# An attention, softmax-MLP and cosine-MLP kernel: the last 64 keys of a late pair are transposed without padding, and the priorities of its list scheduler get other values

## The chip, the cores and the metric

One core of one Trainium2 chip runs the whole program. The metric is device time in microseconds of one execution. The kernel before took 796.75 us (median of three runs, 796.06 to 797.55).

## What is computed

Three layers in a row, all in float32: causal attention in blocks of 64 (4 batches, 8 heads, 576 positions, head size 64), an MLP with a softmax-weighted activation and a layer norm, and an MLP whose activation is h * cos(h). The weights of the MLPs come as float64.

```python
scores = scale * np.matmul(q, k.transpose(0, 1, 3, 2))
mask = block_i >= block_j                  # blocks of 64 positions
scores = np.where(mask, scores, -1000000000.0)
attn = np.exp(scores - np.max(scores, axis=-1, keepdims=True))
attn = attn / (np.sum(attn, axis=-1, keepdims=True) + 1e-09)
o = np.matmul(attn, v)                     # -> x: 2304 tokens x 512

h = x @ w_in                               # 512 -> 1024
sm = softmax(h)
solu = h * sm
ln = (solu - mean) / np.sqrt(var + 1e-06) * g_ln
y = ln @ w_out                             # 1024 -> 512

h = y @ w2_in                              # 512 -> 2048
out = (h * np.cos(h)) @ w2_out             # 2048 -> 512
```

## The kernel before

**Tiles.** Attention works on pairs of heads. A pair's 576 queries are split in two: a *late* group (the last 320 queries, all 576 keys) and an *early* group (the first 256 queries, 256 keys). There are 8 groups (the four late ones first, then the four early ones, `groups`) of 4 pairs each, 16 late and 16 early pairs in all. A late pair has three units (`trace_unit`, t = 2, 3, 4): two of 128 queries and one, t = 4, that puts the last 64 queries of both heads on 128 partitions, with 576 keys in the free dimension. Each unit is a chain: scores on PE (L495 and L498, or L530 for t = 4), the row maximum on DVE, exponentials on ACT, a normalisation on whichever of three engines (L524), PE transposes of the probabilities (L581, in pieces of up to four 128x128 blocks per PSUM bank), a copy to `eT`; then one product with the values for the pair (`trace_pv`, L606).

For t = 4 the 576 keys are four blocks of 128 and one of 64. The tile `e` is 640 wide, its last 64 columns are set to zero (L537, on POOL or DVE), the fifth block is transposed as 128 columns, and only partitions 0 to 63 of the result are copied out.

The 2304 tokens then go in 18 tiles of 128 through the first MLP: `trace_l1` (L678, 24 matmuls of 512 columns), the activation and norm, transposes (`trace_lnT`, L711), and for each four tiles the second matmul in four parts d (`trace_l2`, L732). The second MLP runs over 5 chunks of tokens and 16 weight tiles in two halves: `trace_h2` (L771), the cosine chain on ACT and DVE (`trace_cos`), `trace_out` (L811). The float64 weights are turned into pairs of float32r tiles by `trace_weight` (ACT, DVE and POOL, POOL's part being L641). Attention output goes into a ring of five token tiles (`xs`, slot n % 5), so attention can be at most five tiles ahead of `trace_l1`.

**What sets the order.** All operations are recorded first. `Scheduler.run` then plays a greedy list schedule with costs that are written beside each operation: whenever an engine is free, it takes the ready operation with the smallest key, and the instructions are issued on each engine in that order. The key is `prio - off`. `prio` comes from a time line (`att_iv`, `tile_pr`, `end1` = 373.8 us worked out from its constants) minus or plus the entries of the table `P`; `off` is taken from `P` too, by engine and kind of work:

```python
if kinds & {"e1", "LN", "yb", "psh", "st"}:
    return P["mlp_pe"] if e == "p" else P["mlp_vec"]
if kinds & {"e", "eT", "us", "rq", "rk", "rv", "xs"}:
    return (P["att_pe"] if e == "p" else P["att_vec"]) - P["att_slope"] * o.prio
```

An attention pair of group gi has `prio = s + l * p / 4 - P["lead<gi>"] - P["pair"][p]`, token tile n has `tile_pr[n] + P["tile"][n]`, part d of the second matmul adds `P["l2"] + P["l2_step"] * d`, the weight tiles of the second MLP have `end1 + P["w2_direct"] + P["w2_step"] * (2 * f + c)`. A tile in SBUF or PSUM is given to an operation when it starts, if a slot is free; matmuls on a spare bank (L953) fill planned gaps in the first 70 us.

Of the kernel before, what the change touches and what calls it, by code (L numbers as in the profile page):

```python
# [10 lines left out]
F32 = mybir.dt.float32  # L11
# [17 lines left out]


P = {
    "stick": 24783.0,
    "tile": [-14359.3, -37985.7, 6113.4, -3055.7, 24465.2, 4623.7, 3526.9, -32896.1, -22525.7, 27230.1, -18199.6, 22478.0, 37632.5, 59648.4, -15097.6, 596.8, -22562.3, -32058.0],
    "pair": [-10908.6, 3875.9, 1648.0, 792.0],
    "weight": {"p": 1.0, "s": 2.385, "v": 2.75, "g": 1.376, "q": 1.0},
    "att_slope": 0.053,
    "att_pe": 74866.7,
    "att_vec": 151894.2,
    "mlp_pe": -14159.9,
    "mlp_vec": 34158.7,  # L40
    "w_in": -10429.3,
    "w_out": 307495.7,
    "w_out_step": 1138.4,
    "w2_direct": 73027.9,
    "w2_step": 12920.1,
    "lead0": 7512.5,
    "lead1": 22625.7,
    "lead2": 8969.7,
    "lead3": -7974.6,
    "lead4": -9446.8,  # L50
    "lead5": -67400.4,
    "lead6": -7144.6,
    "lead7": -13408.6,
    "l2": 5241.5,
    "l2_step": 15170.5,
    "prep": 36287.5,
}


# [12 lines left out]
class Scheduler:  # L72
# [24 lines left out]
    def op(self, engs, fn, r=(), w=(), prio=0.0, port=False, iss=0.0, kind="M"):  # L97


        o = Op()  # L100
        o.engs, o.fn, o.prio, o.port, o.iss, o.kind = engs, fn, prio, port, iss, kind
        o.idx, o.succ, o.pred, o.ready, o.start = len(self.ops), [], [], {}, None
        deps, tiles = set(), []
        for k in list(r) + list(w):
            t = k[0] if isinstance(k, tuple) else k
            if isinstance(t, Lt) and t not in tiles:
                tiles.append(t)
        for k in r:
            if k in self.last_w:
                deps.add(self.last_w[k])  # L110
        for k in w:
            if k in self.last_w:
                deps.add(self.last_w[k])
            deps.update(self.reads.get(k, ()))
        for k in r:
            self.reads.setdefault(k, []).append(o)
        for k in w:
            self.last_w[k] = o
            self.reads[k] = []
        deps.discard(o)  # L120
        o.ndep = len(deps)
        for d in deps:
            d.succ.append(o)
        for t in tiles:
            t.refs += 1
        o.tiles = tiles
        self.ops.append(o)
        return o
# [163 lines left out]
def fused_kernel(ctx: ExitStack, tc: tile.TileContext, qT, kT, vm, vt, w_in, w_out, g_ln, w2_in, w2_out, out):  # L292
    nc = tc.nc
    V, S, G, PE = nc.vector, nc.scalar, nc.gpsimd, nc.tensor
# [7 lines left out]
    op = sch.op  # L302


    def c_s(n, ap=False, acc=False):
        return 0.833 * n + 93 + (93 if ap else 0) + (93 if acc else 0)

    def c_v(n):
        return 1.04 * n + 65
# [48 lines left out]
    ident = const.tile([128, 128], F32, name="ident")  # L358
# [102 lines left out]
    def trace_unit(i, t, prep, eT, prio):  # L461
        gi, p = gp_list[i]
        g = groups[gi][1]
        rq, rk, rv = prep
        q0 = g_q0(gi)
        W = 128 * (t + 1)
        us = Lt("us", [128, 8], F32)
        if g == 0:
            if t == 0:
                first_e[i] = [Lt("e", [128, 2, 128 * x + 128], F32) for x in range(2)]  # L470
            e = first_e[i][t]
        else:
            e = Lt("e", [128, 2, W] if t < 4 else [128, 640], F32)

        row = g == 0
        rows = [slice(64 * h, 64 * h + 64) for h in range(2)]
# [49 lines left out]
        else:  # L526
# [5 lines left out]
            for c in range(2):  # L532
# [1 line left out]
                   [scl[c]], [(us, c)], prio)  # L534
            op({"v": 130}, lambda _: V.tensor_scalar(out=us.ap[:, 2:3], in0=us.ap[:, 0:1], scalar1=us.ap[:, 1:2], scalar2=None, op0=ALU.min),
               [(us, 0), (us, 1)], [(us, 2)], prio, port=True)
            op({"g": 130, "v": 100}, lambda q: (V if q == "v" else G).memset(e.ap[:, 576:640], 0.0), [(us, 2)], [(e, 2)], prio)  # L537
            for c in range(2):
                op({"s": c_s(288, True, True)}, lambda _, c=c: S.activation(
                    e.ap[:, 288 * c:288 * c + 288], scl[c].ap, AF.Exp, bias=us.ap[:, 2:3], scale=1.0, accum_out=us.ap[:, 4 + c:5 + c]),  # L540
# [17 lines left out]
        pieces = []  # L558
        if t < 2:
            src = [(h, 128 * j) for h in range(2) for j in range(t + 1)]  # L560
            o = 0 if t == 0 else 128
            pieces.append(([lambda h=h, a=a: e.ap[:, h, a:a + 128] for h, a in src], [(e, 0), (e, 1)],
                           lambda ps: ps.rearrange("p (h q) -> p h q", h=2), lambda x: x[:, :, o:o + W], (t,)))
        elif t < 4:
            for h in range(2):
                o = 128 * (t - 2)
                pieces.append(([lambda h=h, j=j: e.ap[:, h, 128 * j:128 * j + 128] for j in range(t + 1)], [(e, h)],
                               lambda ps: ps.rearrange("p (j q) -> p j q", q=128),
                               lambda x, h=h, o=o: x[:, h, :].rearrange("p (j q) -> p j q", q=320)[:, 0:t + 1, o:o + 128], (t, h)))
        else:  # L570
            pieces.append(([lambda j=j: e.ap[:, 128 * j:128 * j + 128] for j in range(4)], [(e, 0), (e, 1)],
                           lambda ps: ps.rearrange("p (j h q) -> p j h q", j=4, h=2),
                           lambda x: x.rearrange("p h (j q) -> p j h q", q=320)[:, :, :, 256:320], (4,)))
            pieces.append(([lambda: e.ap[:, 512:640]], [(e, 0), (e, 1), (e, 2)], None, None, (5,)))
        for srcs, rk_, vps, vdst, key in pieces:
            n = len(srcs)
            ps = Lt("psb", [128, 128 * n], F32)

            def f_t(_, srcs=srcs, ps=ps):
                for k, s in enumerate(srcs):  # L580
                    PE.transpose(ps.ap[:, 128 * k:128 * k + 128], s(), ident)  # L581
            op({"p": 109 * n}, f_t, rk_ + [(eT, "a")], [ps], prio, kind="T")
            if vps is None:
                f_p, f_d, m = lambda ps=ps: ps.ap[0:64].rearrange("p (h q) -> p h q", h=2), lambda: eT.ap[0:64, :, 960:1024], 128
            else:
                f_p, f_d, m = lambda ps=ps, vps=vps: vps(ps.ap), lambda vdst=vdst: vdst(eT.ap), 128 * n
            op({"s": c_s(m), "v": c_v(m)}, lambda q, f_p=f_p, f_d=f_d: copy(q, f_d(), f_p()), [ps], [(eT,) + key], prio)
# [273 lines left out]
    for i, (gi, p) in enumerate(gp_list):  # L861
        us = (0, 1) if groups[gi][1] == 0 else (2, 3, 4)
        s_, l_ = att_iv[gi]
        pr = s_ + l_ * p / NPAIR - P[f"lead{gi}"] - P["pair"][p]
        prep = trace_prep(i, pr - P["prep"])
        n = 384 if groups[gi][1] == 0 else 1280
        eT = Lt("eT", [128, 2, n], F32)
        for k, t in enumerate(us):
            trace_unit(i, t, prep, eT, pr + l_ / NPAIR * k / len(us))
        trace_pv(i, prep, eT, pr + l_ / NPAIR)  # L870
# [8 lines left out]
    for n in range(NT):  # L879
        pr = tile_pr[n] + P["tile"][n]  # L880
        e = trace_l1(n, pr)
# [18 lines left out]
    for k in range(len(slots) + LAG):  # L900
        if k < len(slots):
            q, c, f = slots[k]
# [6 lines left out]
        if k >= LAG:  # L909
            q, c, f = slots[k - LAG]  # L910
# [20 lines left out]
    with tc.manual_schedule():  # L931
# [9 lines left out]
        for o in order:  # L941
            for t in o.tiles:
                if t.ap is None:
                    make, k, gate, _ = sch.classes[t.cls][t.slot]
# [42 lines left out]
```

## Time and profile before

| | us |
|---|---|
| median of three runs | 796.75 |
| the profiled execution | 796.97 |
| its span, first to last instruction | 795.2 |
| PE (matmul) busy | 784.4 |
| DVE busy | 588.0 |
| ACT busy | 421.8 |
| POOL busy | 219.2 |

The 1.8 us between span and time of the profiled execution lie outside its instructions. PE's busy time is a union of pipelined matmuls, each recorded longer than the distance to its successor, so a PE that waits 0.1 us between two of them is still shown as busy. For this reason the distance between the starts of two groups of matmuls is read beside the busy share.

### The profile page before, as it was taken

The numbers are of one execution on the slowest core, as the hardware profiler recorded it, in microseconds if no ns is written. First come the engines' busy times: TensorE is split into PE (matmuls) and PEld (weight loads), VectorE is DVE, ScalarE is ACT, GpSimd is POOL, SyncE is SP. The second block draws the span as 40 slices with busy tenths as digits, with TensorE's granted clock in tenths as the row PEclk, the third lists the DMA queues.
The fourth block names the chain that finished last, engine by engine and source line by source line (L and its number), as shares of the span: only waits on it lengthen the run. The fifth ranks groups of instructions, "written<-read, shape, count | busy, mean of one in ns | idle before, by whom it ended". The sixth has DMA issues, their size and how long they took to land.

```text
span 795.2 us, 12231 instructions
## 1 busy us (share of the span) xinstructions
PE 784.4 (99%) x4291; PEld 622.1 (78%) x4291; DVE 588.0 (74%) x1238; ACT 421.8 (53%) x944; POOL 219.2 (28%) x320
## 2 busy tenths in 40 slices
PE   8999999999999999999999999999999999999998
PEld 5566666767888777889887778889988888888996
DVE  6989998664643774689879999667766676767775
ACT  6987997655433784476354555343434333333332
POOL 2675544412111553555634542000000000000000
PEclk9999999999999999999999999999999999999999
DMA  8435433322112221624385423022415032131121
GB/s 284 155 96 193 138 109 127 109 79 68 41 53 99 81 68 40 234 104 146 115 300 207 133 85 127 11 100 75 149 51 196 3 109 78 54 132 43 51 79 41
DMA packets 46030, 86.79 MB, mean 109 GB/s; under 512 B 4240, under 2 KB 18576, under 8 KB 45968
## 3 DMA queue, kind: packets, MB, share of 16 engines
q1 hardware_dynamic: 45968, 86.00, 32.5%
q8 instruction: 34, 0.56, 0.3%
q14 instruction: 28, 0.23, 0.1%
HBM read 67.11 MB, written 18.87 MB: 108 GB/s over the span
## 4 chain that ended last, share of the span: by engine, by line
PE 86%; DVE 4%; DMA 3%; ACT 2%; POOL 2%; issue 1%; SPq 0%; ACTq 0%; POOLq 0%
PE banks L771 22%; PE banks L811 22%; PE banks L732 13%; PE banks L678 11%; PE banks L606 6%; PE banks L581 5%; PE banks L495 4%; DMA rq<-qT 3%; PE banks L530 2%; PE banks L711 2%; POOL e L524 1%; DVE tr L787 1%; DVE gt L336 1%; DMA rw<-w_out 1%; POOL t L641 0%
## 5 line engine op out<-in xcount | busy, mean ns | idle before, releaser
L678 PE MATMUL banks<-w,XS 128*128 128x512 f32 x432 | 110.5, 401 | 0.0
L331 ACT ACTIVATE gt<-ta 128x512 fp32r<-128x512 f32 (+1 forms) x80 | 47.0, 588 | 110.0 <-PE banks L811 72.0
L732 PE MATMUL banks<-LN,w 128*128 128x512 f32 (+1 forms) x480 | 103.8, 372 | 0.0
L732 PEld LDWEIGHTS banks<-LN,w 128*128 128x128 f32 x480 | 83.1, 189 | 15.1 <-DVE LN L336 0.2
L678 PEld LDWEIGHTS banks<-w,XS 128*128 128x128 f32 x432 | 78.0, 188 | 18.6 <-issue 3.4
L811 PE MATMUL banks<-w,gt 128*128 128x512 f32 x378 | 91.8, 390 | 0.0
L641 POOL TENSOR_TENSOR t<-t,rw 128x512 uint32<-128x512 uint32 x45 | 63.8, 1419 | 80.3 <-DVE t L639 21.4
L782 ACT ACTIVATE ta<-banks 128x512 f32<-128x512 f32 (+1 forms) x80 | 44.3, 554 | 77.5 <-PE banks L771 76.0
L811 PEld LDWEIGHTS banks<-w,gt 128*128 128x128 f32 x378 | 70.8, 188 | 14.1
L783 DVE TENSOR_SCALAR ta<-ta 128x512 f32<-128x512 f32 (+1 forms) x80 | 37.1, 463 | 59.3 <-ACT ta L782 59.1
L509 ACT ACTIVATE e<-banks,us 128x384 f32<-128x384 f32 (+3 forms) x128 | 66.3, 530 | 20.0 <-DVE us L506 18.0
L791 ACT ACTIVATE ta<-tr,hpi 128x512 f32<-128x512 f32 (+1 forms) x80 | 53.9, 673 | 37.5 <-DVE tr L789 37.4
L506 DVE TENSOR_REDUCE us<-banks 128x1 f32<-128x384 f32 (+3 forms) x128 | 56.0, 481 | 14.8 <-PE banks L498 11.0
L336 DVE TENSOR_TENSOR gt<-ta,gt 128x512 fp32r<-128x512 f32 (+1 forms) x80 | 54.0, 675 | 16.4 <-ACT gt L331 15.6
L811 PE MATMUL banks<-wa,gt 128*128 128x512 f32 x270 | 65.7, 390 | 0.0
L792 DVE TENSOR_TENSOR ta<-banks,ta 128x512 f32<-128x512 f32 (+1 forms) x80 | 50.8, 636 | 12.3 <-ACT ta L791 11.9
L581 PE MATMUL banks<-ident,e 128*128 128x128 f32 x400 | 58.7, 278 | 1.1 <-POOL e L524 0.7
L524 POOL TENSOR_SCALAR e<-e,us 128x384 f32<-128x384 f32 (+3 forms) x97 | 49.1, 518 | 37.8 <-ACT e L509 20.4
L331 ACT ACTIVATE eT<-banks 128x512 f32<-128x512 f32 (+3 forms) x104 | 50.4, 525 | 16.0 <-PE banks L581 15.3
L811 PEld LDWEIGHTS banks<-wa,gt 128*128 128x128 f32 x270 | 50.5, 188 | 10.1
L581 PEld LDWEIGHTS banks<-ident,e 128*128 128x128 f32 x400 | 45.4, 140 | 16.0 <-POOL e L524 4.5
L787 DVE SCALAR_TENSOR_TENSOR tr<-ta,tr 128x512 f32<-128x512 f32 (+1 forms) x80 | 55.3, 692 | 2.2
(127 smaller groups left out, 1428.9 us busy)
## 6 DMA issues: line engine op xcount, KB each, us to landing
rw<-w_out SPq DMA_DIRECT2D x24, 512.0 KB, 3.6
rw<-w_in SPq DMA_DIRECT2D x22, 512.0 KB, 3.9
yD<-YB SPq DMA_DIRECT2D x16, 512.0 KB, 2.9
wa<-yD SPq DMA_DIRECT2D x7, 1024.0 KB, 7.6
rk<-kT SPq DMA_DIRECT2D x16, 288.0 KB, 3.7
oD<-ob SPq DMA_DIRECT2D x18, 256.0 KB, 2.4
ob<-oD SPq DMA_DIRECT2D x18, 256.0 KB, 3.3
rv<-vm SPq DMA_DIRECT2D x16, 256.0 KB, 2.9
```

Source lines behind the costliest of these rows:

```text
L331: S.activation(dst, src, AF.Copy, scale=1.0 if scale is None else scale)
L336: (V if eng == "v" else G).tensor_tensor(out=dst, in0=src, in1=h.bitcast(F32), op=ALU.subtract)
L506: op({"v": c_v(W)}, lambda _, h=h: V.tensor_reduce(out=us.ap[:, h:h + 1], in_=scs[h](), axis=AX.X, op=ALU.max, negate=True), [keys[h]], [( ...
L509: op({"s": c_s(W, True, True)}, lambda _, h=h: S.activation(e.ap[:, h, :], scs[h](), AF.Exp, bias=us.ap[:, h:h + 1], scale=1.0, accum_out= ...
L524: G.tensor_scalar(out=a, in0=a, scalar1=us.ap[:, 6 + h:7 + h], scalar2=1.0, op0=ALU.mult, op1=ALU.mult)
L581: PE.transpose(ps.ap[:, 128 * k:128 * k + 128], s(), ident)
L641: op({"g": c_g2(512)}, lambda _: G.tensor_tensor(out=t1.ap, in0=t1.ap, in1=lw(), op=ALU.add), [(rw, 0)], [t1], prio)
L678: PE.matmul(h.ap[:, 512 * c:512 * c + 512], lhsT=xs.ap[:, a, kt, :], rhs=w[:, b, 512 * c:512 * c + 512], start=(kt == 0 and a == 0 and b = ...
L732: PE.matmul(y.ap, lhsT=w[:, a], rhs=LN[:, b, kf, s0_:s0_ + len(t), :], start=(kf == 0 and a == 0 and b == 0), stop=(kf == 7 and b == 1))
L771: PE.matmul(ps.ap, lhsT=w[:, a, 128 * kt:128 * kt + 128], rhs=yts[q, c][kt // 2].ap[:, kt % 2, b, :], start=(k == 0), stop=(k == 11))
L787: op({"v": c_v(n)}, lambda _: V.scalar_tensor_tensor(out=r.ap, in0=a.ap, scalar=-TWO_PI_B, in1=r.ap, op0=ALU.mult, op1=ALU.add), [a], [r], ...
L811: PE.matmul(acc[x][1](), lhsT=gt.ap[:, a, 128 * x:128 * x + 128], rhs=w[:, b, 512:1024], start=(f % 8 == 0 and k == 0), stop=(f % 8 == 7 a ...
```

## The change

In the unit t = 4 of a late pair the tile `e` becomes 576 wide, the memset of the padding is dropped, and the fifth block is transposed with its 64 columns only; the transpose then writes partitions 0 to 63 of the bank. Its cost in the list schedule becomes 70 instead of 109. All entries of `P` get other values.

```diff
 P = {
-    "stick": 24783.0,
-    "tile": [-14359.3, -37985.7, 6113.4, -3055.7, 24465.2, 4623.7, 3526.9, -32896.1, -22525.7, 27230.1, -18199.6, 22478.0, 37632.5, 59648.4, -15097.6, 596.8, -22562.3, -32058.0],
-    "pair": [-10908.6, 3875.9, 1648.0, 792.0],
-    "weight": {"p": 1.0, "s": 2.385, "v": 2.75, "g": 1.376, "q": 1.0},
-    "att_slope": 0.053,
-    "att_pe": 74866.7,
-    "att_vec": 151894.2,
-    "mlp_pe": -14159.9,
-    "mlp_vec": 34158.7,
-    "w_in": -10429.3,
-    "w_out": 307495.7,
-    "w_out_step": 1138.4,
-    "w2_direct": 73027.9,
-    "w2_step": 12920.1,
-    "lead0": 7512.5,
-    "lead1": 22625.7,
-    "lead2": 8969.7,
-    "lead3": -7974.6,
-    "lead4": -9446.8,
-    "lead5": -67400.4,
-    "lead6": -7144.6,
-    "lead7": -13408.6,
-    "l2": 5241.5,
-    "l2_step": 15170.5,
-    "prep": 36287.5,
+    "stick": 26451.6,
+    "tile": [-43245.2, -107671.1, -30339.0, -14639.2, -22911.6, 4197.5, -31824.9, -26533.9, -797.8, 49077.2, -9719.6, 28521.2, 35640.7, 57607.5, -32409.5, 12744.3, 18745.8, -13140.0],
+    "pair": [-728.0, 7631.2, 6406.5, 9082.1],
+    "weight": {"p": 1.0, "s": 2.732, "v": 2.775, "g": 1.38, "q": 1.0},
+    "att_slope": 0.104,
+    "att_pe": 87074.2,
+    "att_vec": 82748.2,
+    "mlp_pe": -25868.9,
+    "mlp_vec": -41636.5,
+    "w_in": -13390.0,
+    "w_out": 317764.2,
+    "w_out_step": 30356.0,
+    "w2_direct": 410330.0,
+    "w2_step": 6619.4,
+    "lead0": 9930.6,
+    "lead1": 13443.4,
+    "lead2": -18192.8,
+    "lead3": -900.9,
+    "lead4": 18506.1,
+    "lead5": -39857.0,
+    "lead6": -10385.0,
+    "lead7": -29368.1,
+    "l2": 12436.2,
+    "l2_step": 4011.6,
+    "prep": 28608.8,
 }
...
-            e = Lt("e", [128, 2, W] if t < 4 else [128, 640], F32)
+            e = Lt("e", [128, 2, W] if t < 4 else [128, 576], F32)
...
-            op({"g": 130, "v": 100}, lambda q: (V if q == "v" else G).memset(e.ap[:, 576:640], 0.0), [(us, 2)], [(e, 2)], prio)
...
-            pieces.append(([lambda: e.ap[:, 512:640]], [(e, 0), (e, 1), (e, 2)], None, None, (5,)))
+            pieces.append(([lambda: e.ap[:, 512:576]], [(e, 0), (e, 1)], None, None, (5,)))
...
-            def f_t(_, srcs=srcs, ps=ps):
+            def f_t(_, srcs=srcs, ps=ps, vps=vps):
                 for k, s in enumerate(srcs):
-                    PE.transpose(ps.ap[:, 128 * k:128 * k + 128], s(), ident)
-            op({"p": 109 * n}, f_t, rk_ + [(eT, "a")], [ps], prio, kind="T")
+                    PE.transpose(ps.ap[0:64 if vps is None else 128, 128 * k:128 * k + 128], s(), ident)
+            op({"p": 109 * n if vps else 70}, f_t, rk_ + [(eT, "a")], [ps], prio, kind="T")
```

## Rows read from the trace of the kernel before

**Rows 1.** The page's head and busy times of each engine
```profile
span 795.2 us, 12231 instructions
...
PE 784.4 (99%) x4291; PEld 622.1 (78%) x4291; DVE 588.0 (74%) x1238; ACT 421.8 (53%) x944; POOL 219.2 (28%) x320
```

**Rows 2.** Busy by stage: length, PE, PEld, DVE, ACT, POOL, granted clock, DMA, GB/s
```profile
9.00:30.00 21.00, 20.29 (x152) 12.04 (x154) 19.68 (x55) 19.95 (x56) 9.52 (x18) 1.00 0.77 267
30.00:180.00 150.00, 149.81 (x992) 96.73 (x989) 126.69 (x319) 118.01 (x303) 77.08 (x110) 1.00 0.39 122
180.00:260.00 80.00, 80.00 (x456) 64.28 (x455) 38.49 (x97) 35.31 (x90) 15.11 (x37) 1.00 0.20 65
260.00:320.00 60.00, 59.20 (x429) 44.72 (x428) 37.74 (x122) 42.16 (x135) 27.14 (x66) 1.00 0.24 72
403.00:480.00 77.00, 74.11 (x323) 60.13 (x322) 71.22 (x109) 40.55 (x69) 35.33 (x28) 1.00 0.51 177
480.00:792.00 312.00, 311.44 (x1455) 268.09 (x1454) 221.09 (x411) 117.10 (x208) 4.93 (x4) 1.00 0.23 77
```

**Rows 3.** PE in order of time, second MLP: start, us, line, tile, count
```profile
499.55 2.88 PE L811 MATMUL banks<-wa,gt 128*128 128x512 f32 x12
502.27 2.88 PE L771 MATMUL banks<-wb,w 128*128 128x512 f32 x12
```

**Rows 4.** The longest waits of PE over the span: total, times, longest
```profile
PE banks L771 <- DVE ta L792: 2.9, 4, 1.4
...
PE banks L581 <- POOL e L524: 0.7, 3, 0.4
```

**Rows 5.** PE in order of time: transposes, and matmuls of 256 columns, with successors
```profile
180.07 1.90 PE L581 MATMUL banks<-ident,e 128*128 128x128 f32 x15
181.72 3.02 PE L732 MATMUL banks<-LN,w 128*128 128x512 f32 x12
...
363.43 6.00 PE L732 MATMUL banks<-LN,w 128*128 128x256 f32 x48
369.27 2.91 PE L771 MATMUL banks<-wa,wa 128*128 128x512 f32 x12
```

**Rows 6.** Weight loads grouped by line and shape: rows*columns, busy us, mean ns
```profile
L581 PEld LDWEIGHTS banks<-ident,e 128*128 128x128 f32 x400 | 45.4, 140 | 16.0 <-POOL e L524 4.5 <-issue 2.2 <-ACT eT L331 1.3
...
L606 PEld LDWEIGHTS banks<-eT,rv 128*64 128x64 f32 x384 | 24.8, 136 | 20.5 <-issue 3.1 <-ACT eT L331 1.3 <-DVE e L553 0.5
...
L530 PEld LDWEIGHTS banks<-rk,rq 64*64 64x64 f32 x128 | 6.9, 131 | 8.5 <-issue 3.0 <-ACT eT L331 1.2 <-ACT e L509 0.8
```

**Rows 7.** The padding's memset: engine, count, min/median/max ns, first and last start
```profile
L537 POOL MEMSET e<- x11: 144/151/422, 11.3 to 165.1; 128x64 f32 x11
L537 DVE MEMSET e<- x5: 112/112/112, 19.5 to 135.8; 128x64 f32 x5
```

**Rows 8.** Score matmuls of line 495 alone, by stretch: length, PE busy (count)
```profile
200.00:220.00 20.00, 0.93 (x8) 0.52 (x8) 1.00 0.15 49
220.00:240.00 20.00, 0.00 (x0) 0.00 (x0) 1.00 0.18 64
...
260.00:280.00 20.00, 3.71 (x32) 2.10 (x32) 1.00 0.27 81
280.00:300.00 20.00, 4.68 (x40) 2.67 (x40) 1.00 0.26 74
```

**Rows 9.** PE in order of time among the early pairs, with successors
```profile
269.28 1.60 PE L581 MATMUL banks<-ident,e 128*128 128x128 f32 x6
270.81 0.87 PE L606 MATMUL banks<-eT,rv 128*64 128x256 f32 x8
...
278.18 2.16 PE L581 MATMUL banks<-ident,e 128*128 128x128 f32 x10
280.28 0.93 PE L495 MATMUL banks<-rk,rq 64*128 64x128 f32 x8
```

**Rows 10.** DVE from 403 to 480 us, grouped by line and shape: busy, mean ns
```profile
L787 DVE SCALAR_TENSOR_TENSOR tr<-ta,tr 128x512 f32<-128x512 f32 x12 | 11.4, 954 | 0.1
L639 DVE SCALAR_TENSOR_TENSOR t<-t,rw 128x512 uint32<-128x512 uint32 x13 | 9.2, 704 | 0.1
```

## Prediction

> **What bounds the kernel now.** I read the page's busy times first, then the stages, then PE in order of time where the stages leave a doubt, and last the waits. PE is busy 784.4 of 795.2 us and no other engine passes 74% [rows 1], so the end is set by PE, and only three things can move it: PE's own work, idle time of PE, and starts of PE that come late without showing as idle. The stages tell where these lie [rows 2]. From 480 us to the end PE is busy 311.4 of 312 us, and the groups of twelve 512-column matmuls start 2.72 us apart (502.27 - 499.55, [rows 3]), 227 ns each; nothing is to be won there except by less work, and the change takes none away there. From 30 to 260 us PE is again never idle for more than 0.2 us in sum, although DVE (126.7 of 150 us) and ACT (118.0 of 150 us) are nearly as loaded in its late-pair part up to 180 us. Idle PE stands in three places: 0.71 us from 9 to 30 us, 0.80 us from 260 to 320 us, and 2.89 us from 403 to 480 us [rows 2]; the last of these is, to 0.01 us, the four waits of L771 for DVE's last step of the cosine chain [rows 4]. All that a better order could take out of idle time after the first 9 us is thus 0.7 + 0.8 + 2.9 + some 0.8 elsewhere, about 5 us or 0.6%.
>
> To that come late starts. In a good stretch fifteen transposes take 181.72 - 180.07 = 1.65 us, 110 ns each [rows 5]. Among the early pairs six take 1.53 us and ten take 2.10 us [rows 9], where 0.66 and 1.10 us would do: 0.87 and 1.00 us lost, though the stage shows only 0.80 us idle. So the early pairs' stage loses 1.9 us in these two places, and up to 2.7 us if none of its idle time is the same loss.
>
> **The change part by part: the narrower transpose.** There are 16 late pairs, so 16 single transposes out of 400 [rows 6]. The line's operands show e as the loaded weights (128 rows, 128 columns), the identity as what is streamed, 128 columns before and after. The change halves the loaded columns. What one transpose then costs, no row shows; I bound it. From below: matmuls with 128 loaded columns take 227 ns for 512 streamed columns [rows 3] and 122 ns for 256 (369.27 - 363.43 = 5.84 us for 48, [rows 5]), 0.41 ns per column, which goes on to 70 ns at 128 columns; if the streaming alone counts once the load is short, the transpose goes from 110 to 70 ns and 16 x 40 ns = 0.64 us fall away. From above: loads of 64 columns last 131 to 136 ns against 140 ns for the transposes' [rows 6], so if the pace goes by the load's recorded duration only 4 to 9 ns each, 0.1 us in all, are won. A single transpose also stands at the end of a group, where its load can lie behind the matmul before it; then nothing is won. A loss I exclude, since the streamed columns stay and nothing is added. I take 0.6 us, since 110 ns lies well above the line through the two streamed widths, which says that the load sets it; the ends are 0 and 0.6.
>
> The Trainium skill (TensorE: Matmul & The Clock Gate, LDWEIGHTS) has a load take its columns divided by 1.2 in ns and not depend on the rows; by that 64 columns fewer would save an estimated 53 ns each, 0.85 us in all. The recorded durations differ by 4 to 9 ns only [rows 6], so the trace doesn't bear that size out; no run here shows the pace behind 64 transposed columns.
>
> **The memset.** Sixteen small instructions go: 11 on POOL of 151 ns median, 5 on DVE of 112 ns [rows 7], 1.7 us of POOL (28% busy) and 0.56 us of DVE up to 166 us. They ran beside the exponentials that the transpose waits for anyway, so their cover is ACT's work, and PE gets nothing from them. If that cover were gone the price would be one memset per pair, 2.2 us over the 16. The copy to `eT` reads the same 64 partitions as before.
>
> **The new entries of P.** They move every key, so the whole order can shift; I work out which work they move against which. *The weights of the second MLP*: their keys began at end1 + 73 us and now begin at end1 + 410 us, but all keys of the first MLP and of attention lie below end1 + 73 us either way, and a slot of the second MLP that runs at that time has a smaller key too. They came last before and come last now: cost nothing, gain nothing. DVE carries 71.2 of 77 us from 403 to 480 us [rows 2], because these conversions (L639 and its like, [rows 10]) fill every gap between the cosine steps; that remains, and with it the chance of a cosine step that starts behind one of them. *The start*: the first DMA issues are still the inputs of three pairs (three slots of rq, rk, rv) and then the weights: nothing.
>
> *Early pairs against token tiles* is where the order must change. On PE the key of an early pair p = 2 of group 4 was 200.8 + 21.5 + 9.4 - 1.6 = 230.1, less 74.9 - 0.053 x 230 = 62.7: 167. It becomes 200.8 + 21.5 - 18.5 - 6.4 = 197.4, less 87.1 - 0.104 x 197 = 66.6: 131. Group 5 goes the same way from 268 to 237, group 6 from 238 to 240, group 7 from 279 to 296. The token tiles 8 and 9 go from 215.1 - 22.5 + 14.2 = 207 to 240 and from 271 to 304. So the first half of the early pairs comes some 60 us of keys earlier against the tiles beside them. Before, the stretch from 220 to 240 us has no scores at all and the one from 260 to 300 us has 72 of the early pairs' 128 [rows 8]. In that bunch the transposes wait for their chain [rows 9], while from 180 to 260 us DVE, ACT and POOL are busy 38.5, 35.3 and 15.1 of 80 us [rows 2]. Pairs that come earlier get room on these engines, and tiles that come later remain as matmuls with which PE fills the waits of the rest. The ring of five token tiles limits how far this goes: group 6 writes where tiles 9 and 10 lie, and these come later now. Of the 2.7 us that can be lost there I take half as won: 1.3 us; the ends are minus 2.7 and plus 1.9, a second bunch as bad as the first.
>
> *The 2.9 us of L771's waits*: late pairs and the first MLP leave as much conversion work behind as before, and when it opens hangs on the end of attention, which group 6 and 7 hold where it was. These four waits depend on which DVE step happens to stand before the cosine step (L787 takes 954 ns on average there, [rows 10], against 704 ns for L639, a conversion step of the same width). A new order draws them again. I take a quarter off, 0.7 us; the ends are minus 2.9 and plus 2.9.
>
> **Sum.** 0.6 + 1.3 + 0.7 = 2.6 us off the profiled execution's 796.97 us gives 794.4 us. That execution lies 0.2 us above the median of the runs, 796.75 us, so the forecast is 0.3% below that median. A measurement of this kernel can tell about 0.2%, 1.6 us, from no change.
>
> **The rivals.** *Only the transpose counts*: stalls move from one place to another and sum to the same; the time is 796.97 - 0.6 = 796.4 us, with 795.2 to 798.3 as its range. For it speaks that 30 to 260 us and the 312 us of the second MLP have nothing to give [rows 2, 3]; against it that the bunch of early pairs must break up by the keys above.
>
> *The late pairs starve PE*: slower. The early token tiles move up (tile 1 by 70 us in `P["tile"]`, less 12 by `mlp_pe`) and the weights of the first MLP now come before attention units with prio above 70 us on the vector engines instead of above 140 us, all in the stage where DVE is at 84% and ACT at 79% [rows 2]. Each unit's chain of reduction, exponentials and normalisation then ends later and PE's transposes wait. Today 16 waits of weight loads for POOL's normalisation make 4.5 us [rows 6], 0.28 us each, nearly all hidden behind other matmuls [rows 4]. It decides where PE has no ready matmul of another kind to put in between; if 16 more such waits are then open on PE, 16 x 0.28 = 4.5 us come on top of the 0.6 saved: 800.9 us. For it speaks how near DVE is to full there, against it that PE had idle time of only 0.2 us in the 150 us although DVE was that near.
>
> *Most of the stalls go*: 0.6 + 2.7 + 2.9 + 0.7 from 9 to 30 us, 6.9 us, 790.1 us. Only an order that fits everywhere does that.
>
> *The transpose saves nothing* (its load was hidden): 0.6 us more on each of the above, inside their ranges.
>
> **How the numbers follow.** The forecast, between 791 and 795.2 us, has 0.44; most of the stalls gone (below 791) 0.08; only the transpose 0.26; starving late pairs 0.22. The predicted time is the forecast's. The range goes from 789.5 us (most stalls gone, and 0.6 for what the rows don't show) to 799.5 us, which takes in the slower rival as far as 10 of its 16 waits; some 0.16 are left out above and below. Cases of both signs count, so the forecast's own range is 791 to 795.2 us. Faster by over 0.2%: 0.44 + 0.08 = 0.52; within: 0.26; slower: 0.22.
>
> **What would show it.** The 16 narrow transposes stand as a form of their own with 64 loaded columns, and the next start on PE follows after some 70 ns; 110 would refute the first step. Scores of early pairs between 220 and 260 us, fewer from 260 to 300 us, and ten transposes there in about 1.1 us would show the second. Four or fewer waits of L771 for the cosine chain, below 2.9 us in sum, the third; more of them would mean that the conversions start later than I read from the keys. I am wrong if PE shows idle time between 30 and 180 us, or if the early pairs stay where they were.

## The result: slower by 0.76%, and the profile after

The changed kernel takes 802.5 us (median of four runs, 802.04 to 803.11) against 796.62 us of the kernel before beside it: a ratio of 1.0076, with a 95% interval of 1.0064 to 1.0088. The profiled execution took 802.04 us, 5.07 us more than that of before, and its span 4.9 us more. The page's first lines and the stages of the changed kernel (stretch, length, busy time of PE, PEld, DVE, ACT and POOL, granted clock, DMA share, GB/s):

```profile
span 800.1 us, 12249 instructions
...
PE 785.4 (98%) x4294; PEld 621.8 (78%) x4294; DVE 598.4 (75%) x1258; ACT 415.8 (52%) x918; POOL 214.4 (27%) x314
```

```profile
30.00:180.00 150.00, 148.75 (x988) 97.56 (x988) 122.35 (x301) 109.02 (x275) 76.79 (x99) 1.00 0.37 120
...
260.00:320.00 60.00, 58.62 (x391) 44.50 (x386) 47.47 (x141) 39.53 (x117) 26.41 (x64) 1.00 0.27 84
320.00:403.00 83.00, 80.72 (x425) 68.84 (x424) 71.45 (x121) 49.05 (x79) 36.65 (x36) 1.00 0.30 101
403.00:425.00 22.00, 22.00 (x99) 18.23 (x98) 10.75 (x18) 8.59 (x14) 4.05 (x5) 1.00 0.73 249
425.00:505.00 80.00, 76.50 (x333) 61.71 (x332) 76.26 (x114) 40.72 (x69) 34.89 (x30) 1.00 0.46 165
```

PE's idle time went from 10.8 us [rows 1] to 800.1 - 785.4 = 14.7 us; the other 1.0 us of the longer span lies in busy time. Stage by stage against [rows 2]: 30 to 180 us 1.25 us idle (0.19 before), 260 to 320 us 1.38 (0.80), 320 to 403 us 2.28 (none). Where the weights of the second MLP are converted the kernel before has these two rows:

```profile
403.00:425.00 22.00, 20.62 (x91) 16.81 (x90) 18.86 (x29) 11.13 (x20) 8.47 (x8) 1.00 0.75 269
425.00:505.00 80.00, 78.50 (x344) 63.99 (x344) 74.38 (x118) 41.62 (x71) 31.79 (x24) 1.00 0.34 116
```

So from 403 to 425 us idle time fell from 1.38 us to nothing, and from 425 to 505 us it rose from 1.50 to 3.50 us. Over 320 to 505 us this makes 5.78 us where 2.88 us were: 2.9 of the 3.9 us. Most of it lies before 403 us: from there to 505 us idle time went only from 2.88 to 3.50 us. The longest waits of PE (total, times, longest) say on whom, and answer [rows 4]:

```profile
PE banks L770 <- DVE ta L791: 4.9, 5, 1.8
...
PE banks L710 <- DVE ta L791: 0.8, 1, 0.8
```

L770 is the first matmul of the second MLP (L771 before), L791 the last step of the cosine chain, L710 the transposes of the first MLP. Two of these waits, 0.80 us of L710 at 375.5 us and 1.48 us of L770 at 380.8 us, are the 2.28 us before 403 us. DVE's cosine steps have their usual lengths there (0.42 and 0.68 us); what is new is on ACT. The cosine of the second MLP (L790) now runs between the exponentials of the last token tiles (L682), and at each change from one to the other ACT shows an `ACT_TABLE_LOAD` of 1.28 us. The first of the two waits in order of time:

```profile
372.63 1.28 ACT L790 ACT_TABLE_LOAD   x1
373.93 0.72 ACT L790 ACTIVATE ta<-tr,hpi 128x512 f32<-128x512 f32 x1
374.68 0.69 DVE L791 TENSOR_TENSOR ta<-banks,ta 128x512 f32<-128x512 f32 x1 [1.04 <-ACT ta L790]
375.52 1.06 PE L710 MATMUL banks<-ident,E 128*128 128x128 f32 x8 [0.80 <-DVE ta L791]
```

The changed kernel has five such loads from 352 to 374 us, the kernel before has one after 320 us, at 366 us. The second wait comes after the same delay, with a conversion step (L636) and a copy of the first MLP (L327) ahead of L791 on DVE. This is read from the trace; no run takes away the loads alone.

What else moved is seen in PE in order of time, first of the kernel before, then of the changed kernel (start, duration, line, tile, count):

```profile
397.79 5.38 PE L732 MATMUL banks<-LN,w 128*128 128x512 f32 x23
403.01 2.88 PE L811 MATMUL banks<-wa,gt 128*128 128x512 f32 x12
```

```profile
358.24 5.60 PE L677 MATMUL banks<-w,XS 128*128 128x512 f32 x24
363.68 5.60 PE L770 MATMUL banks<-wa,wa 128*128 128x512 f32 x24
369.12 1.07 PE L810 MATMUL banks<-wa,gt 128*128 128x512 f32 x4
...
413.78 9.68 PE L731 MATMUL banks<-LN,w 128*128 128x512 f32 x42
```

Before, the first MLP's last matmul (L732) ends at 403 us and only then the first `trace_out` (L811) starts. Now the second MLP is at `trace_out` by 369 us, and the first MLP's last part runs until 423 us. With it moves what the memory allows: six of the 20 slots for weight tiles open only when the first MLP's tiles are given up, and four more when its last `trace_l1` (L677) is done, at 363.7 us. POOL's step of the conversions by stretch (length, busy, count; granted clock, DMA share, GB/s), before and then after, shows the gap:

```profile
345.00:369.00 24.00, 4.62 (x5) 1.00 0.35 121
403.00:425.00 22.00, 5.55 (x4) 1.00 0.75 269
425.00:505.00 80.00, 17.53 (x11) 1.00 0.34 116
```

```profile
345.00:369.00 24.00, 1.31 (x1) 1.00 0.07 22
403.00:425.00 22.00, 2.85 (x3) 1.00 0.73 249
425.00:505.00 80.00, 20.17 (x14) 1.00 0.46 165
```

Conversions that had been spread over 345 to 490 us are held up twice, and from 425 to 505 us there are then 14 of them instead of 11.

### The profile page after: what moved, and what is told of

Same layout as the page of the kernel before. It is cut to its first block, busy times and chain, and to the rows that moved or that the text cites. A ratio compares the mean times of both kernels' runs of the same rounds, so it can differ in the third digit from the quotient of the medians.

```text
span 800.1 us, 12249 instructions
## 1 busy us (share of the span) xinstructions
PE 785.4 (98%) x4294; PEld 621.8 (78%) x4294; DVE 598.4 (75%) x1258; ACT 415.8 (52%) x918; POOL 214.4 (27%) x314
## 4 chain that ended last, share of the span: by engine, by line
PE 78%; DVE 12%; ACT 4%; issue 2%; POOL 1%; DMA 1%; SPq 1%; ACTq 0%; POOLq 0%; DVEq 0%
PE banks L810 20%; PE banks L770 19%; PE banks L731 12%; PE banks L677 10%; PE banks L580 5%; PE banks L605 5%; PE banks L495 4%; PE banks L710 1%; PE banks L530 1%; DVE gt L336 1%; DVE tr L786 1%; DVE t L638 1%; DVE tr L784 1%; DVE ta L782 1%; DVE ta L791 1%
## 5 line engine op out<-in xcount | busy, mean ns | idle before, releaser
L677 PE MATMUL banks<-w,XS 128*128 128x512 f32 x432 | 110.0, 401 | 0.0
L810 PE MATMUL banks<-w,gt 128*128 128x512 f32 x432 | 104.6, 390 | 0.0
L731 PE MATMUL banks<-LN,w 128*128 128x512 f32 (+1 forms) x480 | 100.6, 369 | 0.0
L677 PEld LDWEIGHTS banks<-w,XS 128*128 128x128 f32 x432 | 78.1, 188 | 19.7 <-issue 3.9
L810 PEld LDWEIGHTS banks<-w,gt 128*128 128x128 f32 x432 | 80.9, 188 | 16.1
L509 ACT ACTIVATE e<-banks,us 128x256 f32<-128x256 f32 (+3 forms) x128 | 66.4, 529 | 21.8 <-DVE us L506 20.6
L790 ACT ACTIVATE ta<-tr,hpi 128x512 f32<-128x512 f32 (+1 forms) x80 | 53.8, 673 | 36.0 <-DVE tr L788 35.5
L336 DVE TENSOR_TENSOR gt<-ta,gt 128x512 fp32r<-128x512 f32 (+1 forms) x80 | 56.5, 706 | 15.9 <-ACT gt L331 15.3
L770 PE MATMUL banks<-wa,w 128*128 128x512 f32 (+1 forms) x288 | 64.5, 372 | 1.5 <-DVE ta L791 1.5
L524 POOL TENSOR_SCALAR e<-e,us 128x384 f32<-128x384 f32 (+3 forms) x105 | 54.8, 534 | 40.0 <-DVE us L515 23.9
L770 PEld LDWEIGHTS banks<-wa,w 128*128 128x128 f32 x288 | 53.0, 188 | 9.9 <-DVE ta L791 1.9
L580 PE MATMUL banks<-ident,e 128*128 128x128 f32 (+1 forms) x400 | 57.7, 278 | 1.8 <-POOL e L524 1.3
L791 DVE TENSOR_TENSOR ta<-banks,ta 128x512 f32<-128x512 f32 (+1 forms) x80 | 50.9, 636 | 10.6 <-ACT ta L790 10.3
L580 PEld LDWEIGHTS banks<-ident,e 128*128 128x128 f32 (+1 forms) x400 | 44.4, 139 | 15.6 <-POOL e L524 6.2
L331 ACT ACTIVATE eT<-banks 128x512 f32<-128x512 f32 (+3 forms) x95 | 46.2, 532 | 19.8 <-PE banks L580 19.2
L786 DVE SCALAR_TENSOR_TENSOR tr<-ta,tr 128x512 f32<-128x512 f32 (+1 forms) x80 | 53.6, 670 | 2.2
```

What stands on the lines that cost most here:

```text
L331: S.activation(dst, src, AF.Copy, scale=1.0 if scale is None else scale)
L336: (V if eng == "v" else G).tensor_tensor(out=dst, in0=src, in1=h.bitcast(F32), op=ALU.subtract)
L509: op({"s": c_s(W, True, True)}, lambda _, h=h: S.activation(e.ap[:, h, :], scs[h](), AF.Exp, bias=us.ap[:, h:h + 1], scale=1.0, accum_out= ...
L580: PE.transpose(ps.ap[0:64 if vps is None else 128, 128 * k:128 * k + 128], s(), ident)
L677: PE.matmul(h.ap[:, 512 * c:512 * c + 512], lhsT=xs.ap[:, a, kt, :], rhs=w[:, b, 512 * c:512 * c + 512], start=(kt == 0 and a == 0 and b = ...
L731: PE.matmul(y.ap, lhsT=w[:, a], rhs=LN[:, b, kf, s0_:s0_ + len(t), :], start=(kf == 0 and a == 0 and b == 0), stop=(kf == 7 and b == 1))
```

## The experiments

The theory that these rows suggest: the narrower transpose does nothing, and the new order pushes the end of the first MLP behind the first slots of the second, which delays the conversions and squeezes them into the cosine chain; there POOL's part of a conversion makes DVE's steps longer, and PE waits. The rivals: a dearer narrow transpose or a missing memset; a loss in the attention stage; cosine waits that have nothing to do with conversions; or a DVE that is simply full. "Late starts" in the expectations are the distances between the starts of successive matmuls beyond what the same succession usually takes in these traces, summed up where they exceed 0.03 us; before has 4.4 us of them from 345 to 505 us, after 7.9 us. Each ratio is to runs of the kernel before on the same chip.

| kernel | median us | ratio to before | 95% interval |
|---|---|---|---|
| before's order, narrow transposes | 797.79 | 1.0008 | 0.9993 to 1.0023 |
| changed, late conversions | 798.05 | 1.0007 | 0.9997 to 1.0016 |
| changed, old keys of tiles 12 to 17 | 798.54 | 1.0012 | 1.0001 to 1.0023 |
| changed, both | 795.61 | 0.9983 | 0.9975 to 0.9992 |
| changed, POOL's add on 16 columns | 797.36 | 1.0000 | 0.9991 to 1.0009 |
| changed code, old P | 801.03 | 1.0059 | 1.0047 to 1.0072 |
| before's code, new P | 808.37 | 1.0147 | 1.0131 to 1.0162 |
| before, late conversions | 794.07 | 0.9954 | 0.9937 to 0.9971 |
| before, late and dense | 798.77 | 1.0027 | 1.0017 to 1.0037 |
| before, late and thin | 792.75 | 0.9945 | 0.9931 to 0.9960 |

**The narrow transpose alone.** In the kernel before the memset's function is emptied and the transpose narrowed, while the planned costs stay, so that the order of all instructions is kept (the tile's width and the transpose's output are those of the change).

```diff
-            op({"g": 130, "v": 100}, lambda q: (V if q == "v" else G).memset(e.ap[:, 576:640], 0.0), [(us, 2)], [(e, 2)], prio)
+            op({"g": 130, "v": 100}, lambda q: None, [(us, 2)], [(e, 2)], prio)
...
-            pieces.append(([lambda: e.ap[:, 512:640]], [(e, 0), (e, 1), (e, 2)], None, None, (5,)))
+            pieces.append(([lambda: e.ap[:, 512:576]], [(e, 0), (e, 1), (e, 2)], None, None, (5,)))
```

> The kernel before with its own instruction order kept on every engine; only the 16 transposes of the last 64 keys load 64 columns instead of 128 and the 16 memsets of the padding are gone. Theory: in the changed kernel the start of a narrow transpose follows its predecessor by 109 ns and the next start follows as far behind it as behind a wide one (203 ns to scores, 28 to 29 ns to the first MLP's matmuls), so the narrowing is worth nothing: 796.6 us within 0.4. Rival (my prediction's first step): 0.6 us less, 796.0. Second rival: the memsets hid something on DVE or POOL that counts, then more than 1 us less.

Measured 797.79 us against 797.09 us of the kernel before beside it: 1.0008, with no change inside the interval. An effect of 0.6 us (0.08%) could not be told by the time alone; the trace tells it. The weight loads of the two widths in the changed kernel (rows*columns, count, busy, mean ns):

```profile
L580 PEld LDWEIGHTS banks<-ident,e 128*128 128x128 f32 x384 | 43.1, 140 | 15.6 <-POOL e L524 6.2 <-issue 1.9 <-ACT eT L331 0.9
L580 PEld LDWEIGHTS banks<-ident,e 128*64 128x64 f32 x16 | 1.8, 112 | 0.0
```

The load is 28 ns shorter, but in the changed kernel all 16 narrow transposes start 109 or 110 ns after the one before them, and what follows starts 202 to 203 ns later if it is scores and 28 to 29 ns later if it is the first MLP, where nothing else delays it. Behind wide transposes the same successions take 200 to 203 and 26 to 29 ns. The narrowing is worth nothing, neither gain nor loss.

**Which half of the new order costs: late conversions.** In the changed kernel the planner gets one more rule: each half of the weight tiles 8 to 15 of the second MLP, which are needed from about 600 us on, is loaded only behind a given slot k of the second MLP (`w2_late` maps k to tiles; here k = 12 + 1.5 n for the n-th half, gated on slot k - 1).

```diff
-                         after=[(w2_t[j], i, 1) for j in range(8) for i in range(2)] if f >= 8 else ())
+                         after=() if gate is None else [("h2", gate)])
...
+            for f2, c2 in w2_late.get(k, ()):
+                w2_weight(f2, c2, k - 1)
             trace_h2(q, c, f, k, when[k])
```

> The changed kernel with the same rule: the second half's weight tiles converted behind slots 11 to 33 of the second MLP. Theory: the 4.9 us of late starts between 425 and 505 us fall below 1.5 us, the 3.0 us between 345 and 425 us stay, since the first eight weight tiles and the last token tiles work there; 798.5 to 799.5 us. Rival (the waits move with the conversions, or come from the order of the first MLP): 802.5 us within 0.6.

```profile
425.00:505.00 80.00, 80.00 (x355) 66.26 (x354) 61.79 (x104) 37.37 (x63) 12.49 (x12) 1.00 0.48 172
505.00:600.00 95.00, 94.87 (x458) 82.90 (x457) 86.13 (x157) 47.15 (x87) 25.20 (x23) 1.00 0.30 105
```

Measured 798.05 us, 1.0007 where the changed kernel has 1.0076, a little better than expected. From 425 to 505 us PE is not idle at all (3.50 us before the edit) and to 600 us only 0.13 us, although the same conversions still run there, on a DVE that is busy 86 of 95 us. The waits did not move with the conversions. The loss before 403 us stays, as expected: L770 and L710 still wait 1.9 us for L791 there.

**The end of the first MLP.** In the changed kernel the entries of `tile` for the token tiles 12 to 17 are set so that their keys on PE are again those of before.

```diff
-    "tile": [..., 28521.2, 35640.7, 57607.5, -32409.5, 12744.3, 18745.8, -13140.0],
+    "tile": [..., 28521.2, 25923.5, 47939.4, -26806.6, -11112.2, -34271.3, -43767.0],
```

> The changed kernel with other numbers for the token tiles 12 to 17 alone, so that their keys on PE are those of the kernel before (their entries of the table less the difference of mlp_pe). Theory: the first MLP then ends near 400 us instead of 423 us, the second MLP's slots before it no longer wait for the cosine chain between 345 and 425 us, and some 2 to 3 us come back: 799.5 to 800.5 us. Rival (the loss sits in the conversions from 425 to 505 us whatever the first MLP does, or in the attention stage): 802.5 us within 1.

```profile
320.00:403.00 83.00, 83.00 (x437) 71.19 (x436) 62.83 (x109) 43.22 (x72) 39.80 (x42) 1.00 0.43 146
...
425.00:505.00 80.00, 78.30 (x343) 63.97 (x342) 74.21 (x119) 41.02 (x68) 28.64 (x24) 1.00 0.33 114
```

Measured 798.54 us, 1.0012: somewhat more than expected came back. The first MLP ends at 402 us, ACT shows one `ACT_TABLE_LOAD` after 320 us instead of five, the 2.28 us of idle time before 403 us are gone, and from 425 to 505 us 1.70 us are left of 3.50. So the late end of the first MLP costs at its own place and again later, through the conversions that it holds up. With these six tiles back at their old keys, 0.64 of the 0.76% are gone: this is the largest part of the loss.

**Both.**

> The changed kernel with both edits: the old keys for the token tiles 12 to 17 on PE, and the second half's weight tiles converted behind slots 11 to 33 of the second MLP. Theory: the two take away different late starts (345 to 425 us, and 425 to 505 us), so of the 7.9 us of late starts there under 1 us is left and the time is 795 to 796 us, 0.1 to 0.2% below the kernel before; 1.5 us of dearer switches between kinds of matmul stay. Rival (both take away the same waits): 798 us, as with either alone.

```profile
425.00:505.00 80.00, 80.00 (x355) 66.25 (x354) 64.39 (x107) 37.89 (x64) 13.76 (x13) 1.00 0.36 125
```

Measured 795.61 us, 0.9983: as expected, and only 0.24 to 0.29% better than with either alone, since each takes away part of the same waits. It is still slower than the kernel before with late conversions (0.9954), so the new order costs some 0.3% outside this place too. The same pairing weighs the conversions themselves: with late conversions in both, the changed kernel is still 0.53% slower (1.0007 against 0.9954), so they make up only some 0.2 of the 0.76%. Both kernels lose time to them.

**POOL beside DVE, or a full DVE.** A wait in the trace of the changed kernel shows what happens (start, duration, engine, line, shapes):

```profile
450.70 1.63 POOL L640 TENSOR_TENSOR t<-t,rw 128x512 uint32<-128x512 uint32 x1 [3.88 <-ACT ob L331]
451.08 1.81 DVE L336 TENSOR_TENSOR gt<-ta,gt 128x512 fp32r<-128x512 f32 x1
452.41 0.94 POOL L333 TENSOR_SCALAR wb<-t 128x512 fp32r<-128x512 f32 x1
452.80 0.83 DVE L788 TENSOR_SCALAR tr<-tr 128x512 f32<-128x512 f32 x1
...
454.43 0.69 DVE L791 TENSOR_TENSOR ta<-banks,ta 128x512 f32<-128x512 f32 x1 [0.19 <-ACT ta L790]
...
455.17 1.20 PE L770 MATMUL banks<-w,w 128*128 128x512 f32 x4 [1.79 <-DVE ta L791]
```

DVE's L336 takes 1.81 us beside POOL's add (0.68 to 0.69 us where POOL rests) and L788 0.83 us beside POOL's L333 (0.42 us); these sit ahead of L791, and PE stands for 1.79 us. To tell this from a DVE that is merely full, POOL's add for the second MLP's weights is cut to 16 of 512 columns, in the unchanged order; in the other columns the lowest bits of these weights are left out.

```diff
+        m = slice(0, 16 if len(after) or prio > 600000.0 else 512)
-        op({"g": c_g2(512)}, lambda _: G.tensor_tensor(out=t1.ap, in0=t1.ap, in1=lw(), op=ALU.add), [(rw, 0)], [t1], prio)
+        op({"g": c_g2(512)}, lambda _: G.tensor_tensor(out=t1.ap[:, m], in0=t1.ap[:, m], in1=lw()[:, m], op=ALU.add), [(rw, 0)], [t1], prio)
```

> The changed kernel in its own order; in the conversion of the second MLP's weights POOL's integer add (line 640) works on 16 of 512 columns, so these weights come out wrong in their lowest bits. The work of DVE, ACT and PE and the instruction order stay. Theory (a DVE step that runs beside a POOL step takes up to twice as long, and that is what delays the cosine chain): most of the 4.9 us of late starts between 425 and 505 us go, 798.5 to 799.5 us, and the cosine steps there come near the 0.68 us that they take elsewhere. Rival (DVE is simply full with its own steps, POOL only runs beside it): 802.5 us within 0.7.

DVE's steps from 425 to 505 us (count, busy, mean ns), first of the changed kernel, then with the short add, and PE's stages with it:

```profile
L336 DVE TENSOR_TENSOR gt<-ta,gt 128x512 fp32r<-128x512 f32 x13 | 13.4, 1031 | 1.6 <-ACT gt L331 1.5
L786 DVE SCALAR_TENSOR_TENSOR tr<-ta,tr 128x512 f32<-128x512 f32 x13 | 11.2, 859 | 0.1
L784 DVE SCALAR_TENSOR_TENSOR tr<-ta,banks 128x512 f32<-128x512 f32 x13 | 8.8, 677 | 0.1
```

```profile
L336 DVE TENSOR_TENSOR gt<-ta,gt 128x512 fp32r<-128x512 f32 x15 | 10.7, 711 | 3.8 <-ACT gt L331 3.7
L787 DVE SCALAR_TENSOR_TENSOR tr<-ta,tr 128x512 f32<-128x512 f32 x14 | 10.0, 711 | 0.1
```

```profile
320.00:403.00 83.00, 81.08 (x427) 69.13 (x426) 64.93 (x122) 49.15 (x79) 21.79 (x37) 1.00 0.32 107
...
425.00:505.00 80.00, 80.00 (x354) 66.24 (x354) 71.11 (x125) 43.64 (x73) 17.11 (x30) 1.00 0.47 168
```

Measured 797.36 us, 1.0000, more than expected: all 3.50 us of idle time from 425 to 505 us are gone though DVE still does every one of its steps. L336 falls from 1031 to 711 ns and L786 (L787 in that run) from 859 to 711 ns. L784, which takes one of its two inputs from PSUM, had 677 ns beside the same POOL. In this stage the theory holds: POOL's step lengthens DVE's. The Trainium skill (SBUF — State Buffer, Who interferes with whom) says that a DVE instruction with two SBUF inputs contends with a GpSimd (here POOL) instruction that reads SBUF, and that the shared ports are an exclusive lock. The trace agrees: L336 from 451.08 us ends 0.56 us after POOL's add ends at 452.33, somewhat less than its undisturbed length, and L784 isn't touched.

Two limits of this run. Before 403 us 1.92 of the 2.28 us stay, with the five table loads, so POOL is not the cause there. And the short add was not run on the kernel before, whose L787 is lengthened too (954 ns, [rows 10]); what POOL makes of the difference between the two kernels is therefore not measured.

**How much of it is density.** In the kernel before, the same rule with 1.5, 0.9 and 1.9 slots for each half (`int(12 + 1.5 * n)`, `int(12 + 0.9 * n)`, `int(6 + 1.9 * n)`).

> The kernel before, with one more rule for its planner: the weight tiles 8 to 15 of the second MLP (needed from about 600 us on) are loaded and converted one half at a time behind the slots 11 to 33 of the second MLP, some 440 to 560 us, instead of as soon as a slot of memory is free. Theory (DVE, filled with conversions from 403 to 490 us and doubled in single steps by POOL's share of them, makes PE wait): the 3.9 us of late starts between 403 and 480 us fall below 1.5 us, and the time goes to 793.5 to 794.5 us. Rival (the waits come from the cosine chain alone, or go where the conversions go): 796.6 us within 0.5, with the same sum of L771's waits for DVE, only later.

> The kernel before with the second half's conversions put behind slots 11 to 24, at 0.9 slots for each half, so 50 us later than in the kernel before but as dense as there. Theory (it is the density, DVE at over 90% and its steps doubled while POOL works beside it, that makes PE wait): 2 to 3 us of late starts come back and the time is 796 to 797 us. Rival (it was only the neighbourhood of the first MLP's end that was full): as good as the version with 1.5 slots each, 0.4 to 0.5% below the kernel before.

> The kernel before with the second half's conversions behind slots 5 to 33 of the second MLP, 1.9 slots for each half. Theory (thinner is better, the first eight tiles are done by 395 us): under 0.5 us of late starts between 403 and 600 us, 793.5 to 794.2 us, 0.4 to 0.5% below the kernel before, no worse than with 1.5 slots each. Rival (early ones meet the first slots while these are still filling): 1 us or more worse than that version, 795 us.

The stages of the dense version, then of the thin one, and last a stretch of the changed kernel with late conversions (1.5 slots):

```profile
425.00:505.00 80.00, 78.73 (x346) 64.45 (x345) 67.19 (x106) 41.52 (x70) 22.24 (x19) 1.00 0.35 119
505.00:540.00 35.00, 31.84 (x151) 27.15 (x150) 32.60 (x57) 19.96 (x36) 15.30 (x13) 1.00 0.42 150
```

```profile
425.00:505.00 80.00, 80.00 (x355) 66.20 (x354) 65.88 (x111) 38.40 (x66) 17.16 (x16) 1.00 0.32 114
505.00:600.00 95.00, 95.00 (x462) 83.88 (x461) 78.83 (x149) 47.00 (x88) 16.02 (x15) 1.00 0.27 92
```

```profile
505.00:540.00 35.00, 34.97 (x168) 30.39 (x167) 32.85 (x57) 17.69 (x32) 9.40 (x9) 1.00 0.20 65
```

794.07 us at 1.5 slots, within what was expected; 798.77 us at 0.9 slots, some 2 us worse than expected and worse than the kernel before; 792.75 us at 1.9 slots, better than expected. The dense version loses 1.27 us of PE from 425 to 505 us and 3.16 us from 505 to 540 us, the thin one nothing up to 600 us. From 505 to 540 us DVE is busy 32.60 of 35 us in the dense version and 32.85 us in the changed kernel with late conversions, which loses 0.03 us there; POOL is busy 15.30 us in the one and 9.40 us in the other. So it isn't DVE's load that decides but how closely POOL's steps follow each other. The thin version beats both kernels: 0.9945, 0.9931 to 0.9960.

**Old table, new graph, and the other way round.** Two kernels with one part each: the changed code with the old `P`, and the code of before with the new `P`, both planned anew.

> The changed kernel with the old table P: the memset is out of the plan and the narrow transpose is planned at 70 ns, and the order is made anew from the old priorities. Theory (an order from the same table drifts at random once a planned cost changes; the stage from 403 to 490 us is as full of conversions as before): 796 to 801 us, most likely 798, with 3 to 6 us of late starts between 345 and 505 us. Rival (the new values of P are the whole of the loss): 796.6 us within 0.5.

> The kernel before with the new table P alone, padding and memset kept. Theory (the new table moves the last token tiles behind the first slots of the second MLP whatever the padding does): the first MLP ends past 415 us, 5 to 9 us of late starts between 345 and 505 us, 802 to 806 us. Rival (the new values only fit the narrow transpose's planned cost and hurt nothing by themselves): 796.6 us within 1.

The stages that differ, first of the old table on the changed code, then of the new table on the old code:

```profile
30.00:180.00 150.00, 145.67 (x970) 94.77 (x967) 120.46 (x298) 111.77 (x282) 69.77 (x92) 1.00 0.38 118
...
425.00:505.00 80.00, 77.07 (x337) 62.49 (x336) 75.10 (x119) 43.28 (x73) 32.27 (x25) 1.00 0.38 132
```

```profile
180.00:260.00 80.00, 78.15 (x489) 59.92 (x489) 40.80 (x117) 36.41 (x111) 21.57 (x56) 1.00 0.24 76
...
425.00:505.00 80.00, 76.49 (x333) 61.73 (x332) 74.78 (x114) 41.62 (x71) 34.00 (x30) 1.00 0.53 184
```

The old table on the changed code takes 801.03 us, nearly as much as the new one, just above the top of what I expected, and by another way: 4.33 us of PE idle among the late pairs (0.19 before) and 2.93 us from 425 to 505 us. The new table on the old code takes 808.37 us, beyond what I expected: the first MLP ends late again, at 425 us, with 1.50 us idle from 320 to 403 us and 3.51 us from 425 to 505 us, and besides 2.63 us are idle among the late pairs and 1.85 us from 180 to 260 us (none before). So the rival that the values of `P` are the whole of the loss falls: a planned cost of 39 ns less and a missing memset, with an unchanged table, make the planner draw another order, and that alone costs 0.6%. The two parts do not add up, 0.59 and 1.47% against 0.76% together: each combination draws an order of its own.

## Why the prediction was wrong

**Forecast faster by 2.6 us, measured slower by 5.9 us**, outside the range. *The narrow transpose*: the line through two streamed widths did not hold, a term of 0.6 us. The distance of 110 ns isn't set by the load of the 128 columns; with 64 columns it is the same. Of the two ends that I had worked out, 0 was right and I took 0.6. The rule of the Trainium skill (TensorE: Matmul & The Clock Gate, LDWEIGHTS) would have erred further: by it an estimated 0.85 us were to be won, and the loads differ by 28 ns, not 53. *The memset*: nothing, as said.

*The second MLP's weights*: exchanging `w2_direct` and `w2_step` alone in the kernel before leaves the order of instructions on every engine as it was, as the keys said. The keys were right and the conclusion was not: I read from the keys alone that "when it opens hangs on the end of attention". It hangs on memory. Attention ends earlier now (its last L605 ends at 310 us against 318), but the first MLP's end moved from 403 to 423 us, and that is when the last slots for weights open. *This is the step that failed*, the path by which I let the second MLP's weights "cost nothing, gain nothing": I worked out the keys of tiles 8 and 9 and left out those of tiles 15 to 17, which by the same sum move on PE from 339, 331 and 333 to 362, 384 and 364, partly past `end1` = 374, where the second MLP's slots begin. With the old keys of tiles 12 to 17, 0.64 of the 0.76% come back. The term "L771's waits", taken as minus 0.7 us with plus 2.9 as its end, measured plus 2.0 us, five waits of 4.9 us, and 0.8 us in L710's wait. Of these, 2.28 us stand before 403 us, at a place that I had not listed and which the conversions don't explain (1.9 us of them stay with late conversions, and with the short add): there the last token tiles and the cosine take turns on ACT and DVE. From 403 to 505 us, the place that I had in mind, idle time rose by 0.6 us.

*The early pairs* did move as the keys said: line 495 alone, by stretch, shows 24 of their score matmuls from 220 to 240 us and 60 from 260 to 300 us where none and 72 stood [rows 8].

```profile
220.00:240.00 20.00, 2.65 (x24) 1.58 (x24) 1.00 0.14 40
...
260.00:280.00 20.00, 2.90 (x28) 1.58 (x24) 1.00 0.33 96
280.00:300.00 20.00, 3.58 (x32) 2.10 (x32) 1.00 0.13 34
```

But next to nothing was won there: from 260 to 320 us idle time went from 0.80 to 1.38 us, and late starts over 180 to 320 us, counted with the alternation of a pair's two heads taken into account, from 6.2 to 5.8 us. So at most 0.4 of the term's 1.3 us came. That thinning the bunch by a sixth leaves each pair's chain as long as it was is my reading; no run shows it.

*The rivals.* The slower rival named the late pairs and 4.5 us; idle time there grew by 1.06 us, to 1.25 us, which I had named as a sign of being wrong. Its place was the smaller part of this loss, but it is the main one with the old table on the changed code (4.33 us idle). What I had seen and not priced was the row of L787 at 954 ns [rows 10]: I called it chance that a new order draws again, and it is a mechanism with a place, which takes more the closer the conversions stand.

About 1.0 us of the longer span, in PE's busy time, and the 1.06 us among the late pairs I haven't traced to a cause by a run; with the last tiles set right, 0.1 to 0.3% stay open (1.0012 with the old keys alone; 0.9983 against 0.9954 with late conversions).

## What to carry to other kernels

Work that isn't due for 100 us should not be let in as soon as a slot is free: a greedy planner puts it beside the critical chain, and here giving it a due time brought 0.55% on the old kernel, more than any value of the priorities tried here. In a planned order read when memory is given back, not only keys, and do the sum for the last tiles of a stage first. Where two stages come to overlap, count the `ACT_TABLE_LOAD`s: here five of 1.28 us stood where one had. When planned costs change, keep the old order with the new code as one of the variants: it tells what the code is worth apart from the order that happens to be drawn.

## What the runs showed of the hardware

A transpose of 128 partitions by 64 columns of float32 keeps the distance of one by 128 columns, 109 to 110 ns, though its load is recorded with 112 instead of 140 ns. Shortening a POOL step that stands on no path of data to the waiting matmul for a hundred microseconds gave back 3.5 us of PE in 80 us, through the steps of DVE beside it. In the changed kernel from 425 to 505 us L786, with two inputs in SBUF, takes 675 to 686 ns where no POOL step overlaps it and up to 1778 ns beside one; L784, with one input in PSUM, takes 668 to 689 ns either way.
